# Key sums of linear attention with the exponentials of four heads as weights and the values moving

## The chip, the cores and the metric

One core of a Trainium2 chip runs the kernel. The metric is the device time of one execution in microseconds, the median of several runs. The core has five engines that work side by side, each through its own queue in order: TensorE (PE in the profile; its weight loads are listed apart as PEld), VectorE (DVE), ScalarE (ACT), GpSimd (POOL) and SyncE (SP), which here only issues DMA. TensorE writes into PSUM, eight banks of 512 float columns on 128 partitions.

## What is computed

Four layers, A, B, A, B, on 2048 rows of 512 numbers, with 32 heads of 16 dimensions, each on a layer norm and added to its input. Layer A is linear attention with a softmax feature map; layer B is a dilated window of 8 positions, which the change doesn't touch. From the reference, layer A:

```python
pq = jnp.einsum("bhsd,hdf->bhsf", q, w_phi)
pk = jnp.einsum("bhsd,hdf->bhsf", k, w_phi)
phi_q = jnp.concatenate([_softmax(pq, axis=-1), _softmax(-pq, axis=-1)], axis=-1)
phi_k = jnp.concatenate([_softmax(pk, axis=-1), _softmax(-pk, axis=-1)], axis=-1)
kv = jnp.einsum("bhsf,bhsd->bhfd", phi_k, v)
z  = jnp.einsum("bhsf->bhf", phi_k)
num = jnp.einsum("bhqf,bhfd->bhqd", phi_q, kv)
den = jnp.einsum("bhqf,bhf->bhq", phi_q, z)[..., None] + 1e-6
o = num / den
```

`kv` and `z` are sums over all 2048 rows: nothing of `num` and `den` can be done before the last key is in. The key sums are what the change rewrites.

## The kernel before

Rows are cut into four blocks `b` of 512, each of four tiles `t` of 128 rows on the partitions. Names carry the pass `L` (0 or 1, each an A and a B layer) and the block: `a1_03` is pass 0, block 3.

Layer A, by stages. `s_a1`: `mk` and `mv` project keys and values of a tile (four matmuls of 512 columns each, L632 and L644); `ek` takes exponentials of the keys with both signs (L638, ACT) into `Ek`; `ev` copies the values out of PSUM into `vaug` (L202 on DVE or L204 on ACT), which has a column of ones beside the values of each head group, set once by POOL; `t8`, `t4`, `t2`, `t1` (DVE) and `rr` (ACT: logarithm L684 and exponential L685) make the softmax's reciprocal `rk`, and `mul` (L690, DVE) multiplies `Ek` by it. `kv` (L707) then adds to the key sums in one PSUM bank, `kvp`, over all 16 tiles of the pass. `s_a2` projects queries (`mq`, L737), takes their exponentials `Eq` (L745, ACT) and their sums `rS` (`ms`, L753; L759 and L760). `s_akv` turns the key sums into what the queries need: `ZM`, the sums `z` masked by head, one for each pass, and `R`, the blocks `kv` masked by head. `s_a3` forms denominators with `ZM` (`md`, L821; `dr`, L829 and L832, DVE; `ln`, L835 and L836, ACT; `rho`, L840, DVE), spreads them over the rows of a head (`bc`, L847) and multiplies them into `Eq` (L855, DVE). `s_a4` multiplies by `R` (`mo`, L940) and by the output weights (L553).

How `kv` works before: for each tile and each of 16 pairs of heads the weights are `vaug` (32 values and the ones: 33 columns) and what moves is `Ek` of the pair with both signs (64 columns). Two matmuls run beside each other, in the halves of the array's columns (`tile_position=(0, 64 * c)`). The result stands with values along the partitions, so that `s_akv` copies the bank (`kvT`), transposes it in four matmuls (L783), and masks it from there: `z` twice (L792) and `r` (L796). The bank is cleared at the start of each pass by a matmul of zeros (L700).

The order of all work is written out. `stages()` files each step under a stage and an engine, and `_ORDER`, a table of some 1500 numbers, says from which of these files the next step is recorded; each engine then works in the recorded order, and waits where data or buffers need it. `_CHOICE` says for each copy out of PSUM (and each residual) whether DVE takes it or ACT, and `_SLOTS` gives the buffer or bank of each tile.

Of the kernel before, what the change touches and what calls it, by code (L numbers as in the profile page):

```python
# [8 lines left out]
BF16 = mybir.dt.bfloat16  # L9
# [7 lines left out]
P = 128  # L17
NJ = 16
D = 512
# [14 lines left out]
VCH = NB * 8 * DV  # L34
EST = (1, 3)
# [25 lines left out]
8 2 i 2e 3s e3 ce 2p 23 i a 5l i i 9 i i i 5o i i i i 4e e7 1m i 0 3u 3r 0 f i e c j b 2 k 3 4 j o 5q 1m l 3 m  # L61
p 1n 0 i 1 n 1t e4 o 1o q 1m 1p r 0 1m 1u s 1m z 5k z z 5 1m 1r 7 6 z 20 20 7 1q 1s 1t 21 21 t 20 20 1v 22 10
z 22 1t 7 1t 20 1w 22 t 11 24 24 13 u 12 16 12 1t t 15 1t v 12 12 22 x 18 14 1x d w w 1y 2c y 18 18 26 18 2d
1f 2d 2c 1z 2d 24 2d 27 17 19 18 1a 1b 21 1c 1d 22 21 22 39 1e 20 20 22 39 25 2c 3b 3a 3a 1f 3a 2d 3a 2f 2c 1f
1f 39 ch 22 2f 2d 2g 1g 29 1f 2d 1j 2f 2d 7 1h 29 1i 1k 3a 29 2n 29 2i 2n 3c 2o 2o 2o 2k 2o 2k 2q 1l cd 2h 2n
2a 2k 2f 2n 2k 3a 2o 2j 24 2q 2r 2q 2o 2o 2o 29 2y 28 2y 2y 3c 2l 2z 2v 2z 2s 2z 2z 2k 2y 2z 39 36 31 2z 36 2z
3a 3b 36 36 2v 31 2v 37 2v 31 2t 36 2z 36 2b 2b 2b 2b 2m 2m ci 36 36 2m 3a 2w 2m 2v 33 34 32 31 3c 35 2q 3c 36
3b 2x g 2x 2u 2x 30 37 2x 36 38 38 38 38 3i 3c 3h 3c 39 3b 3a 3j 3k 3k 3k 3c 3d 3c 3e 3l 3b 3m 3d 3e 5h 3n 3m
3c 3e 3e 3l 5i 3m 3q 3m 3m 4f 3m 3d 3l 5j 3e 3e 3m 5i 3m 3m 3v 3d 3e 3e bd 5h 5m 5n 5i 5i 5i 3m 3d 3e 7c 5h 7d
5p 5i 5i 5i 5r 3f 3g 3g 5i 3f 3g 5i 3w 3f 3z 3x 3f 3g 5s 3y 7e 40 41 3g 7d 5u 5v 7f 5t 3g 3p 41 42 41 41 44 3g  # L70
43 3g 43 5w 5x 5x 7f 45 46 43 43 47 43 7f 5y 3f 90 47 48 49 3g 4c 91 5x 41 4b 41 41 41 4a 92 5x 4d 60 91 4l 5z
61 5z 93 5z 4q 62 5z 4g 7d 4g 4g 4m 4q 63 ck 5z 7d 4r 93 4i 4l 63 66 64 67 7g 4s 7j 65 7h 7i 4h 4j 7k bo 4n 4q
4q 4u 4w 91 7l 4t 7l 7l 7m 7l 7o 68 7n 7n 4l 7p 3h 7n 7q 4w 93 4v 7n 4v 3o 91 4f 6a 7r 4o 6b 7n 6k 6f 69 4g 4k
4l 7r 6l 7s h 4w 6g 6k 6m 4p 6a 6c 6p 7t 7u 6a 6k 6f 6n 7v 4w 6k 6h 94 6r 6d 4x 4x b2 6r 4x 97 6o 98 4x 95 6f
69 7x 96 99 99 9a 4y 6i 99 7w 9b 6q 9c 6q 9d 9b 9b 99 9e 9b 6r 6a 6e 6f 6j 83 84 d4 6q 7y 9f 7y 9b 6r 6s 6s 6s
6s 9f 9h 9i 4y 9g 4w 8d 80 9j 7z 6t 6t 3t 88 6s 83 89 6t 88 88 88 8a 8b 8f 8c 7y 6r 7x 4x 9l 6u 9k 6u 4y 6u 4w
6q 6u 83 85 83 86 87 81 9r 9w 7y 9w 9s 9x 4v 82 4v 9w 6v 9y 9z 4z a1 6v 4z 6v 6w 4z 8e 6v 4z 6y 9m 6x 6z 70 9n
70 70 71 72 73 70 9m 74 72 72 8e 9m 50 50 50 75 50 9o 72 51 9r 52 76 53 8f 54 55 72 9p 9w 76 8f 79 55 77 7a 9r
9t 55 58 78 7b 9u 55 9r 56 9m 8f 59 8g 57 5a 57 8e 8g a3 8g 8g 57 bz b0 8e 9q 57 9v a0 5b 57 8h a3 5b bz 8h a3
8g 5d c0 5e 5c 5f c0 c0 b0 c0 bz 8h b1 5g b3 b1 8f b0 b1 b3 a2 b1 a4 c0 b1 a4 b1 a3 a4 a2 a4 b4 b5 a5 bz a5 8i  # L80
8i c0 8i a2 b3 a4 a2 c0 bx b6 c0 b3 a5 by bx by by b0 b7 bx by by by a3 8i bx 8j 8j b1 8j 8l a6 8k 8j 8m b1 8n
ap by aq aq ap a6 aq aq 8o 8o 8p by 8r 8o 8o 8q 8s 8q as 8t 8q as ap 8q au as ap a6 8u 8q a7 aq at 8u 8w aq bz
a7 8v a7 aq aq 8x 8y 8z bx a9 a6 a7 a8 b8 aa as ax b8 ab ac ac c0 aw by ad ac ac b8 ax b8 ae be af av ah bb bb
bb b9 ag ae bb b8 bf ae ae c1 ai bc bc ae bc ar be ax bc bc bc bc bc ax ay ai aj ac ak am ac an ac al ac be bm
# [2041 lines left out]
```

## Time and profile before

| | us |
|---|---|
| median of 3 runs | 319.71 (319.48 to 320.14) |
| span of the profiled execution, first to last instruction | 318.1 |
| PE, DVE, ACT, POOL busy in it | 307.7, 295.6, 275.0, 47.2 |
| key sums L707: 512 matmuls, busy | 8.4 |
| transposes of the sums, L783: 8 | 0.8 |
| clearing matmuls, L700: 2 | 0.8 |

The profile is of one execution; the profiled execution's own time is known by its span, 318.1 us, and the runs are timed from outside, so that their median lies 1.6 us above it. Times in the rows are from the span's start. A matmul's length in a row holds its way through the pipeline; how fast they follow each other is seen from their starts. TensorE had its full clock throughout (clock 1.000).

### The profile page before, as it was taken

What the parts mean: (1) busy time and instruction counts of PE and PEld (TensorE: products, weight loads), DVE (VectorE), ACT (ScalarE), POOL (GpSimd) and SP (SyncE); (2) the same over time, 40 slices, a digit from 0 to 9 for tenths busy, and PEclk for the clock granted to TensorE, in tenths of its full rate; (3) what the DMA queues carried; (4) which work ended last, traced back from release to release, by engine and by line L of the source; (5) the groups of instructions that cost most, each with busy time, mean ns of one, the idle gap of its engine ahead of it and who ended that gap; (6) DMA issues with size and microseconds to landing.
All of it is one profiled execution on the core that took longest, in us unless ns stands there. A gap on an engine that the chain in (4) does not pass through costs nothing.

```text
span 318.1 us, 8900 instructions
## 1 busy us (share of the span) xinstructions
PE 307.7 (97%) x3578; PEld 152.9 (48%) x3578; DVE 295.6 (93%) x459; ACT 275.0 (86%) x639; POOL 47.2 (15%) x60
## 2 busy tenths in 40 slices
PE   8999999899999999999999999989999999999994
PEld 4644456445454444444444455544444544444552
DVE  6999996998999999999999999689998999999994
ACT  4999999999898778999999999899999867697751
POOL 6000000000004212000000000033141644045000
PEclk9999999999999999999999999999999999999999
DMA  7977100005794989939894600004289875565664
GB/s 203 358 186 148 36 2 4 2 19 145 165 178 100 156 141 136 144 66 140 145 134 62 69 0 2 4 19 134 59 185 137 140 133 134 105 178 126 158 152 170
DMA packets 45789, 36.37 MB, mean 114 GB/s; under 512 B 30832, under 2 KB 41136, under 8 KB 45744
## 3 DMA queue, kind: packets, MB, share of 16 engines
q1 hardware_dynamic: 45216, 35.75, 56.3%
q8 instruction: 29, 0.48, 0.7%
q14 instruction: 16, 0.13, 0.2%
q10 hardware_dynamic: 528, 0.02, 0.1%
HBM read 11.13 MB, written 3.25 MB: 45 GB/s over the span
## 4 chain that ended last, share of the span: by engine, by line
PE 87%; DVE 5%; ACT 5%; DMA 1%; issue 1%; SPq 0%; DVEq 0%; ACTq 0%
PE PS L967 23%; PE PS L553 18%; PE PS L632 9%; PE PS L644 9%; PE PS L737 6%; PE PS L1128 4%; PE PS L1066 4%; PE PS L1185 2%; DVE Eq L855 2%; PE PS L707 2%; PE PS L940 1%; PE PS L482 1%; PE PS L556 1%; PE PS L1200 1%; PE PS L1082 1%; DMA x<-in_A_x_dram 1%
## 5 line engine op out<-in xcount | busy, mean ns | idle before, releaser
L967 PE MATMUL PS<-xnT,WB 128*128 128x512 bf16 x336 | 76.8, 380 | 0.1
L1059 DVE TENSOR_TENSOR prod<-QT,K 128x4096 bf16<-128x4096 bf16 x28 | 63.4, 2287 | 0.5 <-POOL K L993 0.5
L1121 DVE TENSOR_TENSOR pav<-PT,Vg 128x4096 bf16<-128x4096 bf16 (+1 forms) x29 | 62.9, 2214 | 0.2
L967 PEld LDWEIGHTS <-WB 128*128 128x128 bf16 x336 | 37.3, 114 | 36.4 <-issue 3.3
L745 ACT ACTIVATE Eq<-PS 128x512 bf16<-128x512 f32 x64 | 36.3, 619 | 0.0
L638 ACT ACTIVATE Ek<-PS 128x512 bf16<-128x512 f32 x64 | 35.1, 622 | 0.2 <-PE PS L632 0.2
L553 PEld LDWEIGHTS <-oT 128*128 128x128 bf16 x236 | 21.9, 98 | 26.6 <-issue 1.3
L737 PE MATMUL PS<-xnT,WA 128*128 128x512 bf16 x128 | 32.0, 380 | 0.5 <-DVE s L829 0.3
L578 ACT ACTIVATE sqd<-x 128x512 bf16<-128x512 bf16 x48 | 29.9, 631 | 2.2 <-DVE x L571 2.0
L644 PE MATMUL PS<-WA,xnT 128*128 128x512 bf16 x128 | 31.6, 379 | 0.0
L632 PE MATMUL PS<-WA,xnT 128*128 128x512 bf16 x128 | 31.0, 379 | 0.2 <-ACT WA L204 0.2
L571 DVE SCALAR_TENSOR_TENSOR x<-PS,x 128x512 bf16<-128x512 f32 x46 | 30.2, 684 | 0.7 <-PE PS L553 0.7
L204 ACT CAST oT<-PS 128x512 bf16<-128x512 f32 (+1 forms) x50 | 26.7, 597 | 3.8 <-PE PS L1128 2.1
L553 PE MATMUL PS<-WoA,oT 128*128 128x512 bf16 x128 | 29.8, 380 | 0.0
L553 PE MATMUL PS<-WoB,oT 128*128 128x512 bf16 x108 | 26.5, 379 | 0.0
L204 ACT CAST K<-PS 128x512 bf16<-128x512 f32 x30 | 17.3, 593 | 3.1 <-PE PS L967 1.9
L632 PEld LDWEIGHTS <-xnT 128*128 128x128 bf16 x128 | 12.3, 98 | 15.2 <-issue 1.0
L644 PEld LDWEIGHTS <-xnT 128*128 128x128 bf16 x128 | 12.2, 98 | 14.5 <-issue 0.4
L690 DVE TENSOR_TENSOR Ek<-Ek,rk 128x4096 bf16<-128x4096 bf16 (+1 forms) x10 | 18.6, 1860 | 0.4 <-ACT rk L685 0.4
L737 PEld LDWEIGHTS <-WA 128*128 128x128 bf16 x128 | 11.6, 98 | 14.6 <-issue 1.7
L466 DVE TENSOR_SCALAR xn<-x,rstd,nmr 128x512 bf16<-128x512 bf16 x48 | 18.1, 424 | 0.6
L204 ACT CAST V<-PS 128x512 bf16<-128x512 f32 x26 | 15.2, 596 | 2.6 <-PE PS L967 2.6
(175 smaller groups left out, 505.1 us busy)
## 6 DMA issues: line engine op xcount, KB each, us to landing
Vg<-V SPq DMA_DIRECT2D x112, 131.5 KB, 4.3
Prho<-rd SPq DMA_DIRECT2D x8, 512.0 KB, 6.1
x<-in_A_x_dram SPq DMA_DIRECT2D x3, 512.0 KB, 6.6
WB<-in_B_wqkv_dram SPq DMA_DIRECT2D x3, 512.0 KB, 9.8
out_dram<-x SPq DMA_DIRECT2D x6, 256.0 KB, 2.3
wraw<-in_A_wqkv_dram SPq DMA_DIRECT2D x4, 256.0 KB, 4.5
vd<-Vs SPq DMA_DIRECT2D x2, 272.0 KB, 2.9
x<-in_A_x_dram SPq DMA_DIRECT2D x4, 128.0 KB, 3.4
```

Of the source, the lines that this page charges most:

```text
L204: self.nc.scalar.copy(out=out, in_=in_)
L553: nc.tensor.matmul(y[:], lhsT=lh(t, c), rhs=Wo()[:, c, :], start=(c == 0), stop=(c == NB - 1 and not onpe))
L571: nc.vector.scalar_tensor_tensor(out=xb[:, t, :], in0=T[t][:], scalar=1.0, in1=xb[:, t, :], op0=ALU.mult, op1=ALU.add, **kw)
L578: nc.scalar.activation(out=sqd[:], in_=xb[:, t, :], func=ACT.Square, accum_out=T["ss"][:, t:t + 1])
L632: nc.tensor.matmul(pk[:], lhsT=xnT[:, t, k, :], rhs=self.WA[:, k, D:2 * D], start=(k == 0), stop=(k == NB - 1))
L638: nc.scalar.activation(out=T["E"][:, t, s, :], in_=T["k", t][:], func=ACT.Exp, scale=1.0 - 2.0 * s)
L644: nc.tensor.matmul(pv[:], lhsT=xnT[:, t, k, :], rhs=self.WA[:, k, 2 * D:3 * D], start=(k == 0), stop=(k == NB - 1))
L737: nc.tensor.matmul(pq[:], lhsT=self.WA[:, k, hb * P:(hb + 1) * P], rhs=xnT[:, :, k, :], start=(k == 0), stop=(k == NB - 1))
L745: nc.scalar.activation(out=self.Eq[L, b][s][:, :, hb, :], in_=T[hb][:].rearrange("p (t i) -> p t i", t=4), func=ACT.Exp, scale=1.0 - 2.0 * s)
L967: nc.tensor.matmul(pp[:], lhsT=self.WB[:, k, i * D + c:(i + 1) * D:NB], rhs=xnT[:, :, k, :], start=(k == 0), stop=(k == NB - 1))
L1059: nc.vector.tensor_tensor(out=pr[:], in0=QT[:, c:c + 1, :].to_broadcast([P, NW, TB]), in1=win, op=ALU.mult)
L1121: nc.vector.tensor_tensor(out=pv, in0=PT[:, :, lo:lo + n].unsqueeze(1).to_broadcast([P, NB, 2, n]), in1=vw, op=ALU.mult)
```

## The change

The roles in `kv` are exchanged. The weights are now `Ek` of four heads with both signs (128 columns, the whole array), and `vaug` of the same four heads with a column of ones moves (65 columns). A tile has 8 such matmuls where it had 16. The sums of even and odd groups of four heads go to two PSUM banks, 4 times 65 columns in each; the first matmul into each bank clears it, so that the matmul of zeros goes. The result stands with the exponentials along the partitions, as the queries need it, and the transposes go: `sh` copies a quarter (64 partitions, 4 by 65 columns) at a time into `R`, `z` takes the column of ones out of `R` into `ZM` in one instruction, and `r` masks `R` in place. `mo` takes its 32 columns of weights out of 64. `mask2` becomes `mask4`, and `PHI` moves to a shared buffer. `ek` and `ev` write the new layouts.

`_ORDER`, `_CHOICE` and `_SLOTS` are new throughout, a line of each for all:

```diff
-8 2 i 2e 3s e3 ce 2p 23 i a 5l i i 9 i i i 5o i i i i 4e e7 1m i 0 3u 3r 0 f i e c j b 2 k 3 4 j o 5q 1m l 3 m
+8 2 2e 2p 23 i i a d i i 9 i i i i i i i 4g 1m i 0 0 f i e c 2 3 4 j b k j o 1m 3 l m 1n 0 i 1 1t p o 1o q 1m 0
...
-        self.R = const.tile([P, 8, H], BF16, name="R")
+        self.R = const.tile([P, 2, NB, HQ + 2], BF16, name="R")
...
         def ek(t, s):
             if t == 0 and s == 0:
-                T["E"] = self.big([4, 2, D], "Ek")
-            nc.scalar.activation(out=T["E"][:, t, s, :], in_=T["k", t][:], func=ACT.Exp, scale=1.0 - 2.0 * s)
+                T["E"] = self.big([4, 8, 2, HQ], "Ek")
+            nc.scalar.activation(out=T["E"][:, t, :, s, :], in_=T["k", t][:].rearrange("p (g c) -> p g c", c=HQ),
+                                 func=ACT.Exp, scale=1.0 - 2.0 * s)
...
-            self.copy(dve, T["va"][:, t, :, 0:H], T["v", t][:].rearrange("p (a c) -> p a c", c=H))
+            self.copy(dve, T["va"][:, t, :, 0:HQ], T["v", t][:].rearrange("p (g c) -> p g c", c=HQ))
...
         def kv(t):
             if L not in self.kvp:
-                self.kvp[L] = self.ps()
-            K = self.kvp[L]
-            if b == 0 and t == 0:
-                nc.tensor.matmul(K[:], lhsT=self.kvT[:, 0:P], rhs=self.kvT[:], start=True, stop=True)
-            for r in range(4):
-                for h2 in range(2):
-                    for c in range(2):
-                        q = (2 * c + h2) * 4 + r
-                        a = K[64 * c:64 * c + H + 1, h2 * 256 + r * H:h2 * 256 + r * H + 1]
-                        out = bass.AP(a.tensor, a.offset, [list(a.ap[0]), [P, 2], [1, H]])
-                        nc.tensor.matmul(out, lhsT=T["va"][:, t, q, :], rhs=T["E"][:, t, :, q * H:(q + 1) * H],
-                                         start=(b == 0 and t == 0 and r == 0 and h2 == 0),
-                                         stop=(b == 3 and t == 3), tile_position=(0, 64 * c), skip_group_check=True)
+                self.kvp[L] = [self.ps() for _ in range(2)]
+            for g in range(8):
+                c = g // 2 * KVC
+                nc.tensor.matmul(self.kvp[L][g % 2][:, c:c + KVC], lhsT=T["E"][:, t, g, :, :],
+                                 rhs=T["va"][:, t, g, 0:KVC], start=(b == 0 and t == 0 and g < 2),
+                                 stop=(b == 3 and t == 3), skip_group_check=True)
...
-        def ev(dve):
-            self.copy(dve, self.kvT[:], self.kvp[L][:])
...
-        def tr():
-            T["t"] = pt = self.ps(BF16)
-            for g in range(4):
-                nc.tensor.transpose(pt[:, g * P:(g + 1) * P], self.kvT[:, g * P:(g + 1) * P], self.ident[:])
...
+        def sh(half, s, dve):
+            self.copy(dve, R[HQ * half:HQ * half + HQ, s, :, 0:KVC],
+                      self.kvp[L][half][HQ * s:HQ * s + HQ, 0:NB * KVC].rearrange("p (b c) -> p b c", c=KVC))
...
+            nc.vector.tensor_tensor(out=dst, in0=R[:, :, :, HQ:KVC].to_broadcast([P, 2, NB, 8]), in1=msk, op=ALU.mult)
...
+            v = R[:, :, :, 0:HQ].rearrange("p s b (j d) -> p (s b) j d", d=DH)
+            nc.vector.tensor_tensor(out=v, in0=v, op=ALU.mult,
+                                    in1=self.mask4[:].unsqueeze(1).unsqueeze(3).to_broadcast([P, 8, 4, DH]))
...
-                                         lhsT=self.R[32 * r:32 * r + 32, self.reg(s, hb), :],
+                                         lhsT=self.R[32 * r:32 * r + 32, s, hb, 32 * (r % 2):32 * (r % 2) + 32],
```

(`HQ` is 64, `KVC` is 65.) Where the new order and the new steps meet, ACT in the first pass around the reciprocals of the last keys (L684/L685 before, L687/L688 after: `rr` of block 3) and `sq`, a check on the folded weights (L435), reads before:

```order
L204 CAST vaug<-PS 128x16x32
L745 ACTIVATE Eq<-PS 128x4x128
L684 ACTIVATE s_822<-s_822 128x128
L685 ACTIVATE rk<-s_822 128x256
L745 ACTIVATE Eq<-PS 128x4x128
L435 ACTIVATE sq,okc<-WA 128x2048
L745 ACTIVATE Eq<-PS 128x4x128
L759 ACTIVATE rS<-PS 128x256
L760 ACTIVATE rS<-rS 128x256
L745 ACTIVATE Eq<-PS 128x4x128 x4
L835 ACTIVATE Ds<-Ds,deneps_t 128x128
```

and the same place in the changed kernel:

```order
L206 CAST vaug<-PS 128x8x64
L741 ACTIVATE Eq<-PS 128x4x128 x2
L687 ACTIVATE s_754<-s_754 128x128
L688 ACTIVATE rk<-s_754 128x256
L437 ACTIVATE sq,okc<-WA 128x2048
L741 ACTIVATE Eq<-PS 128x4x128 x2
L206 CAST R<-PS 64x4x65 x2
L755 ACTIVATE rS<-PS 128x256
L756 ACTIVATE rS<-rS 128x256
L741 ACTIVATE Eq<-PS 128x4x128 x2
L822 ACTIVATE Ds<-Ds,deneps_t 128x128
```

Two `Eq` have moved ahead of the reciprocals, `sq` stands right behind these, and the two copies of key sums stand behind `sq` and two more `Eq`; `rS` comes after all of them. A copy of `vaug` has gone to DVE.

DVE in the second pass, from the last but one product of `Ek` (L690 before, L693 after) to the first product of `Eq` (L855, L842), before (`nb`, `nok` and `nf` belong to a check):

```order
L202 CAST vaug<-PS 128x16x32
L690 TENSOR_TENSOR Ek<-Ek,rk 128x2048
L1402 TENSOR_TENSOR nb<-okc,sgn 128x2
L792 TENSOR_TENSOR ZM_123<-PS,maskH 128x2x2x8 x2
L796 TENSOR_TENSOR R<-PS,mask_98 128x256
L829 TENSOR_TENSOR s_3461<-PS,rS 128x256
L832 TENSOR_TENSOR Ds<-s_3461 128x128
L1410 TENSOR_TENSOR nok<-PS,thr 128x2
L1411 TENSOR_REDUCE nf<-nok 128x1
L840 TENSOR_TENSOR rho<-rS,Ds 128x256
```

and in the changed kernel:

```order
L693 TENSOR_TENSOR Ek<-Ek,rk 128x4096
L204 CAST vaug<-PS 128x8x64
L693 TENSOR_TENSOR Ek<-Ek,rk 128x2048
L204 CAST R<-PS 64x4x65 x2
L780 TENSOR_TENSOR ZM_122<-R,maskH 128x2x4x8
L1397 TENSOR_TENSOR nok<-PS,thr 128x2
L1398 TENSOR_REDUCE nf<-nok 128x1
L816 TENSOR_TENSOR s_3200<-PS,rS 128x256
L819 TENSOR_TENSOR Ds<-s_3200 128x128
L784 TENSOR_TENSOR R<-R,mask_98 128x8x64
L827 TENSOR_TENSOR rho<-rS,Ds 128x256
```

The big product of block 2 has come down next to that of block 3, two copies of the key sums stand between it and `ZM`, and the masking of `R` has moved behind `s` and `Ds`.

More of the change, by code (lines that the diff above doesn't have):

```diff
@@ L34 @@
 VCH = NB * 8 * DV
+HQ = 4 * DH
+KVC = HQ + 1
 EST = (1, 3)
@@ L221, in constants @@
         self.indB = const.tile([P, NB, 8, DH], BF16, name="indB")
-        self.PHI = self.const.tile([P, NB, 8, DH], BF16, name="PHI")
         self.maskE = const.tile([P, 2, 16], BF16, name="maskE")
```

152 lines of the change are left out of this document (73 added, 79 removed).

## The prediction

> **What bounds the kernel now.** First the page: busy times, and the share of each engine on the chain that ended last.
>
> ```profile
> span 318.1 us, 8900 instructions
> PE 307.7 (97%) x3578; PEld 152.9 (48%) x3578; DVE 295.6 (93%) x459; ACT 275.0 (86%) x639; POOL 47.2 (15%) x60
> PE 87%; DVE 5%; ACT 5%; DMA 1%; issue 1%; SPq 0%; DVEq 0%; ACTq 0%
> ```
>
> TensorE is the bound on the average, but stages may differ, so the second view is the busy time of each engine by stretches: from the first pass's end to the second pass's key sums (67.6 to 194 us), and around those sums.
>
> ```profile
> 67.60:194.00 126.40, 126.39 (x968) 59.67 (x969) 123.71 (x169) 116.35 (x277) 9.32 (x13) 1.00 0.70 113
> 194.00:219.00 25.00, 22.44 (x573) 12.78 (x571) 20.90 (x45) 22.38 (x50) 5.26 (x2) 1.00 0.17 46
> ```
>
> Columns are length, then PE, PEld, DVE, ACT, POOL. In the first stretch TensorE works 126.39 of 126.40 us: nothing else can be its bound, and no other order can win there. Around the key sums of the second pass 2.6 us of TensorE are idle, and DVE and ACT idle too: there the three wait for each other. The change sits in these sums, so next I read TensorE in order of time in both passes. Columns: start, length of the piece, engine, line, operation, count; in brackets idle time before it.
>
> ```profile
> 42.40 1.89 PE L644 MATMUL PS<-WA,xnT 128*128 128x512 bf16 x8
> 44.13 0.38 PE L700 MATMUL PS<-kvT 128*128 128x512 bf16 x1
> 44.44 2.05 PE L707 MATMUL PS<-Ek,vaug 128*33 128x64 bf16 x128
> 46.42 1.90 PE L644 MATMUL PS<-WA,xnT 128*128 128x512 bf16 x8
> 48.16 1.03 PE L737 MATMUL PS<-xnT,WA 128*128 128x512 bf16 x4
> 49.11 2.10 PE L707 MATMUL PS<-Ek,vaug 128*33 128x64 bf16 x128
> 51.15 0.63 PE L753 MATMUL PS<-Eq,indS 128*32 128x128 bf16 x32
> ...
> 52.58 0.39 PE L783 MATMUL PS<-ident,kvT 128*128 128x128 bf16 x4
> 52.81 1.03 PE L737 MATMUL PS<-xnT,WA 128*128 128x512 bf16 x4
> ...
> 194.84 0.38 PE L700 MATMUL PS<-kvT 128*128 128x512 bf16 x1
> 195.15 2.05 PE L707 MATMUL PS<-Ek,vaug 128*33 128x64 bf16 x128
> 197.13 1.90 PE L737 MATMUL PS<-xnT,WA 128*128 128x512 bf16 x8
> 198.86 1.03 PE L644 MATMUL PS<-WA,xnT 128*128 128x512 bf16 x4
> 199.92 0.88 PE L707 MATMUL PS<-Ek,vaug 128*33 128x64 bf16 x48
> 200.73 1.90 PE L644 MATMUL PS<-WA,xnT 128*128 128x512 bf16 x8
> 202.56 1.35 PE L707 MATMUL PS<-Ek,vaug 128*33 128x64 bf16 x80
> 204.59 0.40 PE L783 MATMUL PS<-ident,kvT 128*128 128x128 bf16 x4 [0.68 <-ACT kvT L204]
> ```
>
> Starts count here, not lengths, since a piece ends with its pipeline: eight 512-column matmuls take 197.13 to 198.86, so 0.216 us each. The third view is ACT in the first pass and DVE in the second.
>
> ```profile
> 44.71 0.63 ACT L685 ACTIVATE rk<-s 128x512 bf16<-128x512 f32 x1 [0.20 <-DVE Ek L690]
> 45.25 1.54 ACT L204 CAST vaug<-PS 128x512 bf16<-128x512 f32 x3
> 47.49 0.59 ACT L204 CAST vaug<-PS 128x512 bf16<-128x512 f32 x1 [0.21 <-PE PS L644]
> 52.82 2.14 ACT L745 ACTIVATE Eq<-PS 128x512 bf16<-128x512 f32 x4
> 55.30 0.40 ACT L835 ACTIVATE Ds<-Ds,deneps_t 128x128 f32<-128x128 f32 x1 [0.35 <-DVE Ds L832]
> ...
> 205.03 0.29 DVE L792 TENSOR_TENSOR ZM<-PS,maskH 128x32 bf16<-128x32 bf16 x2 [1.99 <-PE PS L783]
> 206.12 0.42 DVE L829 TENSOR_TENSOR s<-PS,rS 128x256 f32<-128x256 f32 x1 [0.47 <-PE PS L821]
> 207.68 0.43 DVE L840 TENSOR_TENSOR rho<-rS,Ds 128x256 bf16<-128x256 f32 x1 [0.55 <-ACT Ds L836]
> ```
>
> In the first pass these three are ACT's only waits near the key sums, 0.76 us together: it is as full as TensorE, and the logarithm L835, on which `rho` and all products of `Eq` hang, comes when ACT has worked off what stands before it. In the second pass DVE stands still for 1.99 us for the transposed sums. So the same saving of TensorE should be worth little in the first pass and much in the second.
>
> **The change part by part.** *Key sums.* Per pass 256 matmuls (33 weight columns, 64 moving, two at a time in halves of the array) become 128 (128 weight columns, 65 moving, whole array). One row of the trace is near the new form: full weights, loaded anew each time, 64 moving columns.
>
> ```profile
> 261.18 0.63 PE L1193 MATMUL PS<-xnT,WB 128*128 128x64 bf16 x16
> 261.64 1.03 PE L1200 MATMUL PS<-WB,xnT 128*128 128x512 bf16 x4
> L1193 PEld LDWEIGHTS <-WB 128*128 128x128 bf16 x16 | 0.6, 98 | 0.2
> ```
>
> 16 in 0.46 us are 28.8 ns each; with 65 columns 29.2, so 3.74 us a pass. Before: 1.98 (44.44 to 46.42) and 2.04 (49.11 to 51.15), 4.02 together, in the first pass; in the second 1.98, 0.81 and, for the last 80 at 15.5 ns, 1.24, so 4.03. The arithmetic alone saves 0.3 us a pass: two half arrays at 64 columns were already worth nearly one full one. Beside it go the clearing matmul L700, 0.31 us to the start of its follower; some edges between tile forms (four matmuls from 48.16 end at 49.02, the sums start at 49.11, so 0.09 each; two a pass that nothing inherits, 0.2); and the four transposes L783, 0.23. That is 1.0 us of TensorE a pass.
>
> *From the last key sum to the masked sums `ZM` and the matrix `R`.* Gone: one copy of 128x512, the transposes, two `z` and an `r` of 256 columns. New: four copies of 64 partitions by 260 columns (two on ACT, two on DVE), one `z` of 64 columns, one `r` of 512. Nearest rows:
>
> ```profile
> L204 ACT CAST oT<-PS 128x256 bf16<-128x256 f32 x2 | 0.6, 376 | 1.7 <-PE PS L1128 1.7
> L829 DVE TENSOR_TENSOR s<-PS,rS 128x256 f32<-128x256 f32 x8 | 3.4, 420 | 1.6 <-ACT Eq L745 0.8 <-PE PS L821 0.5 <-ACT rS L760 0.3
> L792 DVE TENSOR_TENSOR ZM<-PS,maskH 128x32 bf16<-128x32 bf16 x4 | 0.6, 186 | 3.1 <-PE PS L783 3.1
> L274 DVE TENSOR_TENSOR PHI<-phis,maskH 128x512 bf16<-128x512 bf16 x1 | 0.7, 658 | 0.0
> L745 ACT ACTIVATE Eq<-PS 128x512 bf16<-128x512 f32 x64 | 36.3, 619 | 0.0
> L638 ACT ACTIVATE Ek<-PS 128x512 bf16<-128x512 f32 x64 | 35.1, 622 | 0.2 <-PE PS L632 0.2
> ```
>
> A copy is 0.38 us on ACT and 0.42 on DVE (the `s` row, also 256 float columns from PSUM), some 0.05 to 0.08 less behind another of its kind. That only half the partitions take part, and that two copies move to other partitions, I take as free; the ends are 0.19 (the small `ZM` row) and 0.62 (a whole bank). `z` is between the 0.19 of half its size and 0.42; I take 0.22. `r` is 0.66 by the `PHI` row, which has its 512 columns and its kind of mask; its other end is the 0.42 of 256 columns.
>
> Second pass, from the last key sum at 203.9 to `s` at 206.12: 2.2 us. Now two DVE copies 0.42 + 0.34, `z` 0.22, the sums with `ZM` about 0.6 and four hand-overs of 0.05: 1.8. It saves 0.4, and between 0.0 and 0.8 with the ends of the copies. ACT's two copies run beside DVE's two; ahead of them on ACT stand `Eq`s (0.53 each, a quarter of the four at 52.82) that don't hang on the key sums. `r` now stands behind `s` and `Ds`, in DVE's wait of 0.55 us for ACT's logarithm; 0.1 us stick out, and delay `rho`. Second pass: 1.0 + 0.4 = 1.4 us. DVE's last product of `Ek` may become the later end of the sums; then part of this stays away (next part).
>
> First pass: here ACT decides. Counted in the two orders, up to L835 ACT loses three copies of `vaug` (1.54 together) and gains one (0.51), two new copies (0.76) and a copy of 1024 columns of `xnT` that DVE did (as two of `vaug`, 1.0): +0.7 us. Its 0.76 us of waits can shrink to nothing. So L835 comes 0.06 us earlier at best and 0.7 later at worst; I take no shift, since TensorE, freed by 1.0 us, feeds ACT sooner. That 1.0 us becomes waiting there. `r` lies between `ZM` and `s` on DVE beside TensorE's 0.6 us with `ZM`: covered; were the cover gone, 0.24 us more than the old `r`.
>
> *At no cost.* The exponentials of keys are now written in pieces of 64 columns: `Eq` is written in pieces of 128 at 619 ns, `Ek` in one piece at 622, so nothing, with 0.1 us per pass as either end. The tree of sums and the product L690 see the same contiguous data. `PHI` moves to a shared buffer, `mask4` is one small reduction that replaces another.
>
> *The new order.* Where TensorE is 126.39 of 126.40 us busy, another order can only lose. What can be counted are its changes of tile form, as at 49.11: 93 in the old order, 10 of them at key sums; 89 in the new. So 6 more elsewhere, at 0.09 us 0.5 us, mostly where the logits of the second layer B are broken up. The ends are 0 and, if at each TensorE also waited for one DVE row of 0.42, 3 us, which I hold for unlikely.
>
> **Sum**, against the profiled execution: 318.1 - 0.0 - 1.4 + 0.5 = 317.2 us of span. The median of the three runs, 319.71, lies 1.6 us above this span; with the same around it **318.8 us**, 0.3% faster.
>
> A page speaks against the change. The Trainium skill, "TensorE: Matmul & The Clock Gate", section "LDWEIGHTS (loading the stationary operand)", prices a load by its columns, columns / 1.2 ns: 107 ns for 128, 28 for 33. If loads set the pace, by that page 512 loads of 28 ns would become 256 of 107, an estimate of 13 us more. Row L1193 speaks against that: 16 such loads passed in 0.46 us.
>
> **The rivals.** A row of the waits, on which the second turns (total, times, longest):
>
> ```profile
> PE PS L847 <- DVE rho L840: 2.6, 4, 1.0
> ```
>
> - *Swallowed.* TensorE saves its 2 us, but DVE's last `Ek` product ends the second pass instead, and the order gives back the rest: 319.7 (319.1 to 320.3). For it: DVE is at 93%. Against: it idles 1.99 us just there. That the change doesn't do what it says belongs here: if the whole-array form is no quicker than the half, only L700 and the transposes go, and the 0.5 us of the order bring me within 0.2% of before.
> - *More.* TensorE's waits for `rho` (row above) lie in the same two stages, and all was ordered anew; were half of them to go too, 1.3 us: 317.5. Against: `rho` hangs on DVE's row of products, which hasn't shortened.
> - *Slower by PSUM.* The key sums now hold two of the eight banks from the first sum to the copies. With six left TensorE falls into step with ACT: two `Eq` per bank are 1.07 us (2.14 / 2) against 0.86 for four matmuls, 0.21 lost on each of the 13 projections that the new order puts into the two windows, 2.7 us: 321.5, 1.8 slower than before. It decides once TensorE must be six banks, 5.2 us, ahead of ACT. Against: what it computed from 42.40 on was copied from 45.25 on, a lead of about 3 us.
> - *Slower by weights.* The loads don't hide, since `Ek` changes with each matmul: 256 times the 98 ns of row L1193 is 25 us against 7.5, so 336. Against: the same row's pace.
>
> **How the numbers follow.** 0.2%, 0.64 us, is about what a measurement of this kernel can tell from no change. Forecast (318.0 to 319.4) 0.42, of which 0.04 fall within 0.2%; more, 0.12; swallowed 0.22; slower by PSUM, or by a misfit of the new order of that size, 0.21; slower by weights 0.03. Faster 0.50, same 0.26, slower 0.24. The range goes from 316.8 (half a microsecond under "more", as much as the ends of the copies) to 321.0 (most of the PSUM rival, and the forecast with the order's 3 us).
>
> **What would show it.** Right: key sums about 29 ns apart, 3.7 us a pass; no L700 and no transposes; in the second pass DVE idle before `ZM` under 1.5 us, and 1.4 us less from the first key sum to `s`; in the first pass L835's counterpart near 55.3 us and a TensorE that waits more. Wrong: sums 40 ns or more apart; TensorE waiting for ACT on projections between 40 and 55 us; new waits of TensorE between 67 and 194 us.

## The result, and the profile after

| | before | after |
|---|---|---|
| median, us | 319.92 (4 runs, 319.48 to 320.46) | 323.51 (4 runs, 322.08 to 324.27) |
| ratio, 95% interval | | 1.0108 (1.0087 to 1.0130) |
| span of the profiled execution, us | 318.1 | 320.3 (its time 322.08) |

The change makes the kernel 1.1% slower, 3.6 us; 318.8 was predicted, and 321.0 was the upper end. The profiled execution is the fastest of the four, so its trace shows 2.2 us of the 3.6. First the page of after: busy times, and the chain by engine.

```profile
span 320.3 us, 8376 instructions
PE 307.4 (96%) x3312; PEld 153.0 (48%) x3312; DVE 296.6 (93%) x459; ACT 275.9 (86%) x643; POOL 44.9 (14%) x60
PE 72%; DVE 12%; ACT 9%; DMA 3%; issue 2%; SPq 0%; DVEq 0%; ACTq 0%
```

TensorE is as busy as before (307.7) although it runs 266 matmuls fewer, and its share of the chain fell from 87 to 72%: it waits more. Two stretches answer to those shown of before (length, then PE, PEld, DVE, ACT, POOL).

```profile
68.50:195.00 126.50, 125.89 (x962) 59.08 (x963) 121.05 (x161) 117.58 (x279) 15.35 (x16) 1.00 0.69 113
195.00:220.00 25.00, 22.34 (x444) 13.67 (x443) 22.66 (x48) 22.89 (x53) 7.49 (x5) 1.00 0.13 34
```

Between the passes TensorE now idles 0.61 us where it idled 0.01, and around the second pass's key sums 2.66 us instead of 2.56. Next TensorE in order of time in both passes (start, length of the piece, operation, count, idle time before it).

```profile
46.76 1.18 PE L703 MATMUL PS<-vaug,Ek 128*128 128x65 bf16 x32
47.78 1.02 PE L733 MATMUL PS<-xnT,WA 128*128 128x512 bf16 x4
...
49.76 2.20 PE L703 MATMUL PS<-vaug,Ek 128*128 128x65 bf16 x64
51.89 0.63 PE L749 MATMUL PS<-Eq,indS 128*32 128x128 bf16 x32
52.45 1.04 PE L733 MATMUL PS<-xnT,WA 128*128 128x512 bf16 x4
54.68 0.63 PE L808 MATMUL PS<-Eq,ZM 128*32 128x128 bf16 x32 [1.19 <-DVE ZM L780]
...
202.55 2.96 PE L703 MATMUL PS<-vaug,Ek 128*128 128x65 bf16 x88
205.35 0.16 PE L1393 MATMUL PS<-nb,ones 128*128 128x2 bf16 x1
205.44 0.63 PE L749 MATMUL PS<-Eq,indS 128*32 128x128 bf16 x32
206.81 0.63 PE L808 MATMUL PS<-Eq,ZM 128*32 128x128 bf16 x32 [0.73 <-DVE ZM L780]
```

The clearing matmul and the transposes are gone, but 32 key sums take from 46.76 to 47.78, 31.9 ns each and not 29.2, and in both passes TensorE waits for `ZM`, 1.19 us in the first. Why that one is so long stands in ACT's and DVE's rows of the first pass, and then DVE's of the second.

```profile
51.42 1.06 ACT L741 ACTIVATE Eq<-PS 128x512 bf16<-128x512 f32 x2
52.51 0.77 ACT L206 CAST R<-PS 64x260 bf16<-64x260 f32 x2
...
56.22 0.40 ACT L822 ACTIVATE Ds<-Ds,deneps_t 128x128 f32<-128x128 f32 x1 [1.25 <-DVE Ds L819]
```
```profile
53.31 0.43 DVE L204 CAST R<-PS 64x260 bf16<-64x260 f32 x1 [1.83 <-ACT R L206]
53.66 0.18 DVE L302 COPY indDen<-indAV 128x128 bf16<-128x128 bf16 x1
53.87 0.42 DVE L204 CAST R<-PS 64x260 bf16<-64x260 f32 x1
54.40 0.23 DVE L780 TENSOR_TENSOR ZM<-R,maskH 128x64 bf16<-128x64 bf16 x1
...
205.55 0.87 DVE L204 CAST R<-PS 64x260 bf16<-64x260 f32 x2 [1.02 <-PE PS L1393]
206.53 0.23 DVE L780 TENSOR_TENSOR ZM<-R,maskH 128x64 bf16<-128x64 bf16 x1
```

In the first pass DVE is free from 51.5 and the sums are in at 52.0, yet its first copy starts at 53.31, when both of ACT's copies are done: the four run one after another. In the second pass the two engines copy side by side (ACT from 205.51). The logarithm that was at 55.30 now comes at 56.22.

The last place is the end of the program. Two rows of DVE show when the flag `fl` is decided (before, then after), and the view of the transfers, cut to the time from the issue of the last store to its landing, what passed there.

```profile
314.51 0.15 DVE L1429 TENSOR_SCALAR fl<-PS 128x1 int32<-128x1 f32 x1
```
```profile
311.42 0.15 DVE L1416 TENSOR_SCALAR fl<-PS 128x1 int32<-128x1 f32 x1
```

Transfers of before, 314.65 to 316.34 us:

```profile
q1 hardware_dynamic: 292, 0.26, 44.7%
q14 instruction: 1, 0.01, 1.9%
...
out_dram<-x SPq DMA_DIRECT2D x1, 128.0 KB, 1.7
```

Transfers of after, 315.59 to 318.66 us:

```profile
q1 hardware_dynamic: 296, 0.26, 26.7%
q14 instruction: 3, 0.02, 3.1%
q8 instruction: 1, 0.02, 2.6%
...
out_dram<-x SPq DMA_DIRECT2D x1, 128.0 KB, 3.1
```

The same 128 KB land 1.7 us after their issue before, and 3.1 us after it now. The flag says whether the program may end or has to be redone another way; it is read by all engines ahead of a branch. The new order decides it 3 us earlier, and packets of program code (queues of kind "instruction", one of 16 KB that alone takes 1.27 us on its DMA engine, against 46 ns for 1 KB of a store) now travel among those of the store. (The one such packet in the view of before starts 0.01 us ahead of the landing.) In the trace of before every 1 KB of the last stores takes 44 to 46 ns. In that of after some beside the code take 72 to 253 ns, and the last ones follow each other singly, about 43 ns apart, until 318.15.

Two accounts of the trace, summed over all its rows. TensorE from the start of each matmul to the start of the next, by step: key sums 9.45 to 8.27 us and transposes 0.46 to 0, so 1.64 saved; logits of layer B (`lgt`) 13.02 to 14.00, query projections 29.72 to 30.53, sums of `Eq` with the wait for `ZM` behind them 4.96 to 5.69, key projections 28.11 to 28.61, `mo` 5.71 to 6.04, and smaller ones: 2.57 lost. So the last matmul starts at 314.72 instead of 313.79, 0.93 later. From there to the end it takes 5.62 us instead of 4.33, another 1.28.

### The profile page after: what moved, and what is told of

The parts are those of the page before. It is cut to its first block, busy times and chain, and to the rows that moved or that the text cites. A ratio compares the mean times of both kernels' runs of the same rounds, so it can differ in the third digit from the quotient of the medians.

```text
span 320.3 us, 8376 instructions
## 1 busy us (share of the span) xinstructions
PE 307.4 (96%) x3312; PEld 153.0 (48%) x3312; DVE 296.6 (93%) x459; ACT 275.9 (86%) x643; POOL 44.9 (14%) x60
## 4 chain that ended last, share of the span: by engine, by line
PE 72%; DVE 12%; ACT 9%; DMA 3%; issue 2%; SPq 0%; DVEq 0%; ACTq 0%
PE PS L954 21%; PE PS L555 16%; PE PS L647 4%; PE PS L634 4%; PE PS L733 4%; PE PS L1115 4%; PE PS L1053 4%; ACT Ek L640 3%; PE PS L1172 2%; DVE Eq L842 2%; DMA Prho<-rd 2%; DVE s L668 2%; DVE Ek L693 1%; PE PS L927 1%; PE PS L703 1%
## 5 line engine op out<-in xcount | busy, mean ns | idle before, releaser
L640 ACT ACTIVATE Ek<-PS 128x512 bf16<-128x512 f32 x64 | 35.9, 630 | 0.0
L647 PE MATMUL PS<-WA,xnT 128*128 128x512 bf16 x128 | 32.1, 379 | 0.0
L634 PE MATMUL PS<-WA,xnT 128*128 128x512 bf16 x128 | 31.4, 379 | 0.6 <-ACT WA L206 0.6
L580 ACT ACTIVATE sqd<-x 128x512 bf16<-128x512 bf16 x48 | 30.3, 649 | 0.7 <-DVE x L573 0.3
L996 POOL COPY vh<-V 128x64 bf16<-128x64 bf16 x6 | 12.6, 2092 | 50.2 <-ACT V L206 26.7
L206 ACT CAST QT<-PS 128x512 bf16<-128x512 f32 x27 | 16.1, 596 | 3.4 <-PE PS L954 3.3
L693 DVE TENSOR_TENSOR Ek<-Ek,rk 128x4096 bf16<-128x4096 bf16 (+1 forms) x10 | 18.6, 1860 | 0.2 <-ACT rk L688 0.2
```

Of the source, the lines that this page charges most:

```text
L206: self.nc.scalar.copy(out=out, in_=in_)
L580: nc.scalar.activation(out=sqd[:], in_=xb[:, t, :], func=ACT.Square, accum_out=T["ss"][:, t:t + 1])
L634: nc.tensor.matmul(pk[:], lhsT=xnT[:, t, k, :], rhs=self.WA[:, k, D:2 * D], start=(k == 0), stop=(k == NB - 1))
L640: nc.scalar.activation(out=T["E"][:, t, :, s, :], in_=T["k", t][:].rearrange("p (g c) -> p g c", c=HQ), func=ACT.Exp, scale=1.0 - 2.0 * s)
L647: nc.tensor.matmul(pv[:], lhsT=xnT[:, t, k, :], rhs=self.WA[:, k, 2 * D:3 * D], start=(k == 0), stop=(k == NB - 1))
```

## The experiments

Edits of the order are shown as recorded steps: engine, stage, step, arguments. `sh(half, s)` is one of the four copies of the key sums, from bank `half`. Each ratio is to runs of before on the same chip (medians 319.89 to 320.06).

**Order or sums.** Two crossings come first: the new sums in the old order, and the old sums in the new order.

```diff
 PE  a1_03 kv(3)
-DVE akv0 ev
+DVE akv0 sh(1,0)
+DVE akv0 sh(1,1)
 ACT bound sq(0)
+ACT akv0 sh(0,0)
+ACT akv0 sh(0,1)
...
-PE  akv0 tr
-DVE akv0 z(0)
-DVE akv0 z(1)
+DVE akv0 z
 DVE akv0 r
```

> The new key sums, copies, `z` and `r`, in the order of before: where the copy of the transposed form stood, the four copies stand (DVE takes both of the second bank, ACT both of the first); the transposes are left out; the buffers are those of before, but that the second bank of the key sums moves five other tiles to other banks. Theory 'order' (the sums are sound, the loss is made by places of the new order): TensorE keeps its 1.6 us less in `kv` and transposes, of which the second pass passes on 0.7 to 1.2 us and the first nothing, so 318.7 to 319.4 us against 319.9 of before, ratio 0.996 to 0.999. Theory 'sums' (32 ns a sum, four copies and two banks cost more than they bring wherever they stand): as slow as the changed kernel, 322 us or more, ratio above 1.006.

Measured: 319.97 us, ratio 0.9999 (0.9989 to 1.0009). Neither theory holds as it was put: the sums do no harm, and they bring nothing. In its trace the logarithm of the first pass comes at 55.52 (55.30 before), and `s` of the second at 206.22 (206.12).

The second crossing is the reverse, with `ev` and `tr` in the places of the copies, in the order of the change:

```diff
-DVE akv0 sh(0,1)
+DVE akv0 ev
...
-DVE akv0 sh(1,0)
+PE  akv0 tr
-DVE akv0 z
+DVE akv0 z(0)
+DVE akv0 z(1)
```

> The key sums of before (33 weight columns, 64 moving, one copy, transposes, two `z`, `r`) in the order of the change, with its engines and buffers. Theory 'order': it is slow without the new sums as well, 323 to 325 us, ratio 1.010 to 1.016, since to the losses of the order come the 1.6 us of TensorE that the old sums take more, in part. Theory 'sums': back at before, 319.5 to 320.5 us, ratio 0.999 to 1.002.

Measured: 325.66 us, ratio 1.0179 (1.0162 to 1.0195), even above the 1.016 expected. The loss belongs to the new order and not to the sums; in it the new sums are worth 0.7%, in the old one nothing. This kernel loses in part at other places than the changed one: no copies are crossed here, and yet its logarithm of the first pass comes at 56.52, behind the transposes, and its last matmul starts 2.90 us later than before. Where the rest of the 2.90 arises stays open.

**The copies in a row.**

```diff
 ACT a2_01 eq(3,1)
-ACT akv0 sh(1,1)
+ACT akv0 sh(0,1)
 ACT akv0 sh(0,0)
-DVE akv0 sh(0,1)
+DVE akv0 sh(1,1)
 DVE c_ind_den ind_den
 DVE akv0 sh(1,0)
```

> The changed kernel with two of the first pass's four copies exchanged: ACT takes both of the first bank, DVE both of the second, in the places of before the exchange, so that DVE's first copy no longer waits for ACT's. Theory 'copies in a row': DVE copies at 52.0 instead of 53.31 us, ACT's two end at 53.3 as they did, `ZM` follows at 53.4 instead of 54.40, and the logarithm in front of `rho` comes 0.9 to 1.0 us earlier (55.3 instead of 56.22), as does all behind it: 0.9 us less than the changed kernel, 322.6 us, ratio 1.008. Rival 'swallowed': TensorE's place in the order is taken up by the wait at 103 us for the product behind the transfer `Prho`, or by another one: within 0.3 us of the changed kernel, ratio 1.010 to 1.012.

Measured: 321.80 us, ratio 1.0057 (1.0035 to 1.0079). DVE and ACT of this kernel in the first pass:

```profile
51.96 0.43 DVE L202 CAST R<-PS 64x260 bf16<-64x260 f32 x1 [0.52 <-PE PS L701]
52.41 0.20 DVE L300 COPY indDen<-indAV 128x128 bf16<-128x128 bf16 x1
52.62 0.42 DVE L202 CAST R<-PS 64x260 bf16<-64x260 f32 x1
53.32 0.23 DVE L778 TENSOR_TENSOR ZM<-R,maskH 128x64 bf16<-128x64 bf16 x1 [0.28 <-ACT R L204]
```
```profile
55.13 0.40 ACT L820 ACTIVATE Ds<-Ds,deneps_t 128x128 f32<-128x128 f32 x1 [0.21 <-DVE Ds L817]
```

The rows are as expected, to 0.2 us: DVE copies from 51.96, `ZM` comes at 53.32, the logarithm at 55.13, even earlier than before the change. The time fell by more than expected: 1.7 us, where 0.9 was forecast, while the logarithm comes 1.09 earlier. TensorE's last matmul starts at 313.61, earlier than before the change too; all that is left of the loss lies behind it. In the program of the change DVE's first copy carries a wait for ACT, which the exchange takes away:

```
after:  L204 CAST R<-PS 64x4x65 [waits PE_49,Activation_49]
here:   L204 CAST R<-PS 64x4x65 [waits PE_49]
```

So it is a wait that the program holds. It stands where two engines read one bank; here each engine reads its own, and the wait is gone. (The exchange also changes which rows of `R` each engine writes; the two were not tried apart.) The Trainium skill, "PSUM — Partial Sum Buffer", section "PSUM bank collisions raise a hardware error", says to guard PSUM by bank and quadrant of 32 partitions, or, simpler, by bank. ACT's and DVE's copies lay in different quadrants; by the finer rule they might have run beside each other, and if it is the bank that the wait guards, the program behaves as by the simpler one.

**The flag.** Three kernels: the exchanged copies with a late flag, the kernel of before with an early one, and the changed kernel with only the flag late.

```diff
-DVE flag decide
 ACT b3_11o res(2)
...
-ALL flag read
...
 ACT b3_12o res(3)
 SP  b3_12o store(2,3)
+DVE flag decide
 SP  b3_12o store(3,4)
+ALL flag read
```

> The kernel of the exchanged copies (321.8 us) with the flag's last steps put where the order of before has them: `decide` on DVE and its reading by all engines behind the last products, beside the last store, instead of ten steps earlier. Theory 'code load': with the flag known early the engines run on to what stands behind the branch while the last stores are still on their way, and the code for it (packets of 8 and 16 KB, 0.6 to 1.9 us each on one DMA engine, at 314.5 to 316 us) holds up store packets of 1 KB (46 ns): the last two stores need 3.7 to 4.1 us from issue to landing instead of 1.7. Then 1.3 to 1.9 us go: 319.9 to 320.5 us, ratio 0.9995 to 1.0015. Rival 'large stores late' (the two stores of 256 KB that the new order issues just ahead of the last four take the time): nothing changes, ratio 1.005 to 1.007.

Measured: 319.87 us, ratio 0.9995 (0.9981 to 1.0009): 1.9 us less by these two steps alone. Flag and transfers from the last store's issue to its landing (314.75 to 316.43 us):

```profile
314.60 0.15 DVE L1414 TENSOR_SCALAR fl<-PS 128x1 int32<-128x1 f32 x1
```
```profile
q1 hardware_dynamic: 295, 0.27, 45.4%
...
out_dram<-x SPq DMA_DIRECT2D x1, 128.0 KB, 1.7
```

No packet of code is among them; the first starts at 316.51. With the flag early (exchanged copies alone, 314.48 to 318.18 us) it looked so:

```profile
q1 hardware_dynamic: 309, 0.28, 22.7%
q8 instruction: 1, 0.02, 3.2%
q14 instruction: 3, 0.02, 2.5%
...
out_dram<-x SPq DMA_DIRECT2D x1, 128.0 KB, 3.7
```

The reverse, in the kernel of before:

```diff
 PE  b3_12o mm(0)
+DVE flag decide
...
-DVE flag decide
+ALL flag read
 SP  b3_12o store(3,4)
-ALL flag read
```

> The kernel of before, `decide` moved ahead to the step behind the flag's sum and the reading ahead of the last store; nothing else is changed. Theory 'code load': the tail of before gets longer by 1.0 to 1.9 us as in the changed kernel, 321.0 to 322.0 us, ratio 1.003 to 1.006. Rival 'large stores late': the same as before, ratio 0.999 to 1.001.

Measured: 321.77 us, ratio 1.0051 (1.0038 to 1.0065). `decide` and the reading, moved by a few steps in an otherwise unchanged kernel, cost 1.8 us. In its trace POOL and TensorE read the flag at 312.24 and go through the branch, TensorE by 313.24; a packet of 16 KB of code runs from 314.08 to 315.72; SP's issue of the last store but one takes 1.92 us instead of 0.33, and the last store is issued at 316.83 instead of 314.65. So it is the same cause, but here it holds up the issue and not the landing. Part of the 1.8 us is another: in this kernel SP itself reads the flag ahead of the last store (from 316.14, 0.55 us), in that of before behind it.

Which engine's branch the packet belongs to can be read from the times: in all 14 traces the last packet of 16 KB begins 0.65 to 1.04 us after TensorE has gone through its branch, and no other engine's branch is followed by it at so steady a distance. In the changed kernel TensorE is through at 315.13, 0.46 us ahead of the last store's issue; before, at 315.69, 1.04 behind it.

> The changed kernel (323.5 us, ratio 1.0108) with only the flag's two last steps put behind the last products, as in the order of before; the first pass's copies stay as they are. Theory 'two causes that add up': the flag takes 1.8 to 2.2 us, by the pair with and without it (321.8 and 319.87), so 321.3 to 321.7 us, ratio 1.0040 to 1.0055. Rival 'one cause': the wait of the copies counts only through the end of the program, so that either edit alone brings all: ratio below 1.002.

Measured: 321.91 us, ratio 1.0054 (1.0036 to 1.0073). The two causes add up: mending the flag alone brings 0.54%, the copies alone 0.51%, both 1.13%.

This run's trace also shows one reason why the executions of the changed kernel lie farther apart (322.08 to 324.27 us) than those of before (319.48 to 320.46). From 11 to 88 us it runs some 0.2 us behind the trace of after. Then the second read of `Prho` for the fourth block lands 7.78 us after its issue instead of 6.41, DVE waits 2.23 us for it instead of 0.93, TensorE goes on with layer B's projections at 104.57 instead of 103.04, and its last matmul starts at 316.26 instead of 314.72. The trace with sums by bank (below) has it too: 7.59 us, last matmul at 315.89. So with the copies crossed the last matmul is 0.9 to 1.1 us later than before in three traces and 2.1 to 2.5 in two, and the median price of 1.6 to 1.7 us lies between. What lengthens the read, and whether the late first pass makes that more frequent, no run shows.

The flag against the end of the program in seven traces:

| | `fl` decided | last store issued, landed | us | 16 KB of code begins |
|---|---|---|---|---|
| before | 314.51 | 314.65, 316.34 | 1.69 | 316.44 |
| after | 311.42 | 315.59, 318.66 | 3.07 | 315.93 |
| old sums, new order | 313.39 | 317.92, 320.49 | 2.57 | 316.44 |
| new sums, old order | 314.19 | 314.34, 316.02 | 1.68 | 316.13 |
| exchanged copies | 310.31 | 314.48, 318.18 | 3.70 | 314.75 |
| the same, flag late | 314.60 | 314.75, 316.43 | 1.68 | 316.51 |
| after, flag late | 316.98 | 317.13, 318.83 | 1.70 | 318.91 |

**The pace of the key sums.** Three kernels, one execution each (322.45, 322.54 and 323.80 us), of which only the pace is read: one column fewer, half the columns (both leave values out of the sums), and another sequence of banks.

```diff
-nc.tensor.matmul(self.kvp[L][g % 2][:, c:c + KVC], lhsT=T["E"][:, t, g, :, :],
-                 rhs=T["va"][:, t, g, 0:KVC], start
+nc.tensor.matmul(self.kvp[L][g % 2][:, c + 1:c + KVC], lhsT=T["E"][:, t, g, :, :],
+                 rhs=T["va"][:, t, g, 1:KVC], start
```

> The changed kernel with 64 moving columns in each key sum instead of 65: the first value column of each four heads is left out of the sums (the ones column stays), so its entries of `R` are what the bank held. Theory 'odd width' (the 65th column, and with it places in the bank that start at odd columns, cost more than 1/65): 28.8 ns a sum as in L1193, 3.7 us a pass. Rival 'pace of the form' (new weights of 128 columns in strides, two banks in turn): 31.5 ns a sum or more, 4.0 us a pass.

The mean distance of neighbouring starts stays at 31.8 ns: not the odd width. With 33 in the place of 1, so that 32 columns move:

> The changed kernel with 32 value columns and the ones column moving in each key sum... that is 33 columns less one: columns 33 to 64 of 65; the first 33 value columns of each four heads are left out of the sums. Theory 'weights set the pace': 31.8 ns a sum as with 65 and 64 columns. Rival 'moving columns set it': half, 16 to 20 ns.

It falls to 25.6 ns. That is between the two theories: weights do not set the pace at 64 columns, and half the columns do not halve it.

```diff
-for g in range(8):
+for g in (0, 2, 4, 6, 1, 3, 5, 7):
```

> The changed kernel with the eight key sums of a block of tokens in another sequence: the four of the first bank, then the four of the second, instead of in turn. Theory 'banks in turn cost': 28.8 to 29.5 ns a sum as in L1193, whose sums stay in one bank. Rival 'weights set the pace': 31.8 ns.

It falls to 30.2 ns. The rows of 32 sums with 32 columns, and then of 32 sums by bank:

```profile
47.13 0.96 PE L703 MATMUL PS<-vaug,Ek 128*128 128x32 bf16 x32
47.94 1.02 PE L733 MATMUL PS<-xnT,WA 128*128 128x512 bf16 x4
```
```profile
46.93 1.13 PE L703 MATMUL PS<-vaug,Ek 128*128 128x65 bf16 x32
47.90 1.03 PE L733 MATMUL PS<-xnT,WA 128*128 128x512 bf16 x4
```

0.81 us / 32 is 25.3 ns, 0.97 / 32 is 30.3. That looks like a price of changing the bank, but the distances one by one don't bear it out. In the changed kernel every sum goes to the other bank than the one ahead of it; still 64 of 248 distances are 29 or 30 ns, all of those behind the first and the fifth sum of a tile, and the others 32 to 35. With sums by bank, 192 distances stay within a bank and 55 change it: their means are 30.3 and 30.1 ns. There the slow ones stand behind the second and the sixth sum of a tile (32.4 and 32.7 on average), where the bank does not change. So the sequence matters and the bank is not what makes it matter; what does stays open. The Trainium skill, "TensorE: Matmul & The Clock Gate", section "Back-to-back issue gap", gives a floor of about 25 ns for matmuls of up to 64 columns; the 25.6 ns at 32 columns agree with it. The 29.1 ns of L1193 at 64 columns lie above that floor.

**Two attempts at more, and a miss.** On SP, in the kernel with copies exchanged and the flag late:

```diff
+SP a3_03 rdb(0)
+SP a3_03 rdb(1)
 SP a4_01o tr
...
-SP a3_03 rdb(0)
-SP a3_03 rdb(1)
```

> The kernel with exchanged copies and late flag, and on SP the two reads of `Prho` for the fourth block of 512 tokens (86.78 and 87.76 us) put ahead of the transposing transfer of `xn` that waits until 84.65, so that they start at about 80.7, when their source has landed. Theory 'queue': DVE's wait of 0.83 us for `Prho` at 94.11 goes, with it TensorE's 0.44 us for `oT` at 101.86: 0.4 to 0.8 us less than without it, ratio lower by 0.0013 to 0.0025. Rival 'cover': DVE catches up or TensorE is bound by its own row, within 0.2 us of the kernel without it.

Measured: 323.83 us, ratio 1.0114 (1.0096 to 1.0132), worse by 4 us. The reads couldn't start at 80.7, since their buffer came free at 84.6; the transposing transfer, now behind 1 MB of them, landed at 94.01 instead of 89.24, and TensorE waited 2.6 us for what hangs on it. I had looked at the source and not at the buffer.

In the old order with the new sums:

```diff
-ACT akv0 sh(0,0)
-ACT akv0 sh(0,1)
+DVE akv0 sh(0,0)
+DVE akv0 sh(0,1)
...
+PE  a3_00 md
 PE  a2_02 mq(0)
-PE  a3_00 md
```

> The new sums in the order of before (319.97 us), with three edits: the first pass's four copies all on DVE (ACT loses 0.75 us, DVE, which waits 1.59 us there, gains it); the first sums with `ZM`, and the logarithm behind them, one projection earlier, `r` behind `s`; and in both passes the two tiles that had got a bank of the key sums (0.41 and 0.97 us of TensorE's waiting) get another one. Theory 'ACT decides in the first pass': the logarithm at 55.52 comes 0.7 us earlier, and all of layer B behind it; in the second pass 0.3 us: 318.9 to 319.3 us, ratio 0.9965 to 0.998. Rival 'DVE decides': between 58 and 67 us DVE is busy for 9.41 of 9.44 us, so the earlier start is lost again: ratio 0.999 to 1.001.

Measured: 320.74 us, ratio 1.0017 (1.0006 to 1.0028), slower than without the edits. It is neither rival: TensorE now stands 0.65 us before the sums with `ZM`, and the projection behind them comes late, so that ACT waits 1.17 us for it. The same without moving `md` and the logarithm, and with `r` behind `s` in the second pass as well:

> The new sums in the order of before (ratio 0.9999), with the first pass's four copies on DVE, `r` behind `s` in both passes, and the two tiles that waited for a bank of the key sums (0.41 and 0.97 us of TensorE) in another one; the sums with `ZM` stay where they stood. Theory 'ACT and the banks held back what the sums bring': the logarithm of the first pass at 55.1 instead of 55.52 us, the second pass 0.3 us shorter, 0.4 to 0.7 us together: 319.2 to 319.6 us, ratio 0.9978 to 0.999. Rival 'nothing left to bring': the sums take TensorE as long as before and DVE closes both passes, ratio 0.9992 to 1.0005.

Measured: 319.64 us, ratio 0.9991 (0.9981 to 1.0000): the lowest of all, 0.25 us below before, at the edge of what can be told from it, and just short of the 0.999 expected. The logarithm of the first pass, expected at 55.1, stands at 55.71 in its trace, but that trace, of the slowest of the 11 executions, is 0.66 us late from the first key sum on (44.80 instead of 44.13); from the last key sum to the logarithm it takes 4.05 us, 0.46 less than without the edits (4.51), as was expected. In its second pass the first key sum and `s` are 11.05 us apart (195.47 to 206.52).

## Why the prediction was wrong

Its main sentence on the order was "Where TensorE is 126.39 of 126.40 us busy, another order can only lose", priced at 0.5 us by changes of tile form. That was read off one stretch. The order also moved steps where TensorE is not the bound, and there it lost 3.6 us at two places. With both mended the new order is worth what the old one is (0.9995 against 0.9999). The 4.7 us between 318.8 and 323.51 are these 3.6, the 0.9 of saving that did not come (steps 3 to 5), and 0.2 by which the median of before rose with its fourth run.

1. *The end of the program.* The step that failed most: "with the same around it **318.8 us**". The working stops at 219 us and takes all behind it, the end of the program too, for given. The order showed `decide` and the reading of the flag some steps earlier; I didn't ask what they release. Price: 1.6 to 1.9 us.
2. *First pass, "I take no shift".* The end of the range was 0.7 us later by ACT's work; the logarithm came 0.92 later, but not by ACT's work: ACT waits 1.25 us ahead of it. What was missed is that wait: "ACT's two copies run beside DVE's two" was said of the second pass, where it held, and taken over for the first, where engines and banks were crossed. Price: 1.6 to 1.7 us; without it the logarithm stands at 55.13 and 55.43 in two traces, where I had put 55.30, so that "no shift" would have held.
3. *Key sums at 29.2 ns, 3.74 us a pass.* Mis-sized: 31.8 ns, 4.08 us in the second pass (0.77, 0.51 and 2.80), against 4.03 before. The row L1193 is the same in weights and columns and ran at 29.1; what else sets these sums apart, the runs above leave open, and it is not the bank. So the arithmetic saves nothing.
4. *L700, transposes, form changes.* Right in kind: `kv` and transposes take 1.64 us less of TensorE in both passes, where 2.0 were predicted. L700 (0.62) and the transposes (0.46) came as said; the sums themselves bring 0.56, where arithmetic and form changes were to bring 1.0, by step 3.
5. *Second pass, 2.2 to 1.8 us, 1.4 in all.* From the last key sum to `s`, counted as in the prediction from the end of the sums' row, it is now 1.98 us (205.51 to 207.49) where 1.8 was predicted: 0.2 saved of the 0.4. The two copies take 0.87 where I put 0.76, and `z`, the sums with `ZM` and the hand-overs 0.1 more together. DVE's wait ahead of the copies fell to 1.02 us, as said. From the first key sum to `s` it is 11.4 us after 11.3 before (with L700): the sign that I had named, 1.4 less, is not there. It was a poor sign, since the new order put 24 projection matmuls into that stretch where 20 stood; these four take 0.86 us, so that for equal work some 0.75 came of the 1.4. With the old order `s` comes at 206.22 against 206.12; there one tile of my own making waited 0.97 us for a bank of the sums, and where it didn't (the last kernel above) the stretch is 11.05 us, 0.2 less than before. TensorE waits 0.80 us for an `Eq` there instead.
6. *The rivals.* For the sums "swallowed" is what happened, for the reason given there ("if the whole-array form is no quicker than the half"): 0.9999. "Slower by PSUM" was the right sign for a wrong reason: two banks for the sums cost nothing in the old order. "Slower by weights" fell: whole-array weights change with each of the 128 matmuls of a pass, at 31.8 ns on average with 65 columns and 25.6 with 32.

What stays open: the 0.98 us more of `lgt` and the 0.61 us of waits between 68.5 and 195 us, which something else in the new order gives back, since the sum of both orders is the same; how much of the wait in step 2 is by bank and how much by the rows of `R`; and why the first pass's wait, 1.1 us by the logarithm, costs 1.6 to 1.7 us of the median: a longer read of `Prho` in some executions is seen, its reason is not.

## What to carry to other kernels

A new order must be read at the places where the busiest engine does *not* work all the time: the end of the program, and hand-overs between engines, above all what a step that moved releases. Here it paid to decide the flag that ends the program behind the last products, and to read it behind the last store's issue. Where two engines empty PSUM together, give each its own bank, as here in the exchanged copies, or look for the wait. And a pace taken from the nearest row is an estimate until it is read in place: sums alike in weights and columns ran at 29 ns and at 32 to 33.

## What the runs showed of the hardware that was not expected

- Packets of program code share the way of the stores: one of 16 KB, begun 0.65 to 1.04 us after TensorE had gone through its branch, took 0.9 to 1.9 us. Begun with or just after the last store's issue, it went with 3.1 to 3.7 us until that store landed instead of 1.7; begun ahead of an issue, with 1.92 us for the issue instead of 0.33.
- Matmuls with 128 weight columns, loaded anew each time, follow each other every 25.6 ns with 32 moving columns. With 65, the distances are 29 ns at some places of a tile and 32 to 33 at others, 31.8 on average in one sequence and 30.2 in another, and the change of bank does not tell which. 64 and 65 columns make no difference (31.8 both).
